# Row scatters given places behind the tiles' q work, and the gate weights' low halves formed on VectorE without a clamp

## The chip, the cores and the metric

The kernel runs on one core of a Trainium2 chip. The metric is the device time of one execution in microseconds (us); a run's time is one execution, and the kernel before has a median of 771.07 us over 3 runs (768.2 to 772.1). All times below come from one profiled execution of that kernel.

## The reference

Three stages follow each other on 3072 tokens of 384 numbers (4 batches of 768 tokens, 8 heads of 48).

```python
# 1. linear attention with decay
f = 1 / (1 + exp(-f_logit))
for t in range(768):
    state = f[:, :, t, :, None] * state + einsum('bhd,bhe->bhde', k[:, :, t], v[:, :, t])
    y[:, :, t] = einsum('bhd,bhde->bhe', q[:, :, t], state)
# 2. a skip score and one expert of 8 (w1: 384 x 1024, w2: 1024 x 384)
do = x @ w_skip > 0
e = argmax(x[do] @ w_gate);  p = its softmax share
out = x;  out[do] = x[do] + p * (relu(x[do] @ w1[e]) @ w2[e])
# 3. RMS norm and a gated layer (384 -> 1536 -> 384)
xn = x / sqrt(mean(x * x) + 1e-6) * rms_g
g = xn @ w_gate2
return (g * sigmoid(g) * (xn @ w_val2)) @ w_out2
```

The three weights of stage 3 (`g_gate`, `g_val`, `g_out` in the kernel) come as 64-bit floats, all else as 32-bit floats.

## The kernel before

Every product that needs 32-bit accuracy in stages 2 and 3 is made of 16-bit halves: a number is a high half (`hi`, `wgh`, `gh`, names in h) plus a low half (`lo`, `wgl`, `gl`, names in l), and TensorE (PE) multiplies hi by hi, hi by lo and lo by hi into one sum.

**Attention, 0 to about 166 us.** 24 tiles of 128 tokens, tile i is chunk i//4 of batch i%4. `tile_ops` lists the steps of a tile. ACT makes the decay factors `en` and `ep`; DVE makes `ks = k*en` and POOL makes `qs = q*ep` (its instruction is kept in the list `scaled`); PE transposes both (`ptk`, `ptq`), ACT copies the results to `Tk` and `Tq`; PE makes the scores `sc` and the output `py`. POOL also decays the running `state`, which ACT copies into `sbd` for `py`. A table of offsets per step and 3.09 units per tile (`II`) order the steps of all tiles in one list; a scheduler that simulates the program then sets the order on each engine, and `tc.issue_after(x)` keeps an instruction behind x in that order.

**Routing.** Tiles go through `route_ops` in groups (4, 4, 4, 4, 4, 2, 1, 1): DVE finds the expert, PE counts ranks (`prk`), DVE writes each token's slot. Then each tile's rows `xh`, with `meta` copied beside them, are scattered to the DRAM buffer `xs` by slot: one indirect DMA on POOL's queue for each tile. The scatters of a group are listed `RS` apart and not before `RS_AT`; for the first 8 tiles tile i's scatter also stands behind the `qs` of tile 10 + (i+1)//2. Every scatter waits for twelve writes of zero rows to `xs` that go out on SP's queue between the attention's loads.

**Experts, about 186 to 330 us.** For each of 8 experts 256 slots are read transposed (`exT`); `ph`, relu to `hh` and `hl`, `ey`. `start(0)` does the first 96 slots of expert 0 (`pa`, `eah`, `eal`) before the last rows are scattered. Two side queues go beside them: weights of later experts, then the gate and value weights of stage 3 (`gates`), and the rows: `first` makes the normalised rows `xn` of blocks 0 and 1 and transposes them by DMA into `xnT`; `middle` and `place` scatter the rest to `xnd`, from which `later` reads them.

**Gate weights.** `prep_in(nm, p)` loads one sixth of `g_gate` or `g_val` (768 KB) as pairs of 32-bit words into a staging buffer `st` (4 of them), makes 32-bit floats of them (`narrow`, with ACT's absolute value and DVE's clamp, shift and two merges into one of 2 buffers `fb`), scales them by `rms_g` (ACT, three pieces of 256 columns), rounds to the high half (ACT) and subtracts for the low half (POOL, line 430). `prep_out` does `g_out`, with the low half on DVE already.

**Gated layer.** Six blocks of 512 tokens and 12 column groups m. `up` makes `pwg` and `pwv` (9 matmuls each), ACT's `sg`, DVE's `hf`, ACT's `gh`, DVE's `gl`; `down` sums `po` over all m. Blocks 0 and 1 go through `pair` side by side, while the rest of the weights is prepared; blocks 2 to 5 through `block`. `bounds` checks that all values stayed inside the ranges that the fast path allows; if not, a slow general path runs behind it.

Of the kernel before, what the change touches and what calls it, by code (L numbers as in the profile page):

```python
# [32 lines left out]
FORCE = False  # L33
NONE = 4096
NPRE = 0
POOL_LO = True
WB = 3
FA = 1
EARLY = 20
# [23 lines left out]
ALT = 0  # L63
ALM = 0
AHM = 1
RS = 4.0
RS_AT = 37.0
CLEAR = 10
GATED = 8
FIRST = 17  # L70
GROUPS = (4, 4, 4, 4, 4, 2, 1, 1)
BUFS = {'xT': 3}
# [15 lines left out]
def fused_kernel(ctx, tc, q, k, v, f, w_skip, w_gate, w1, w2, g_gate, g_val, g_out, rms_g, out, dbg=None):  # L88
# [47 lines left out]
    dec = keep.tile([128, NT, 2 * HP], F32, name="dec")  # L136
    cnt = keep.tile([128, 2 * E + 1], F16, name="cnt")
    osum = keep.tile([128, NT], F32, name="osum")
    big = keep.tile([128, 2 + 2 * E + 3], F32, name="big")

    wr = keep.tile([128, HP, E + 1], F32, name="wr")
# [49 lines left out]
    def narrow(o, lo, hi):


        nc.scalar.activation(out=o.bitcast(F32), in_=hi.bitcast(F32), func=AF.Abs)
        yield
        nc.vector.tensor_scalar(out=o.bitcast(F32), in0=o.bitcast(F32), scalar1=2.0 ** -15 * 1.125, scalar2=2.0 ** 16 * 1.9375, op0=ALU.max, op1=ALU.min)
        nc.vector.tensor_scalar(out=o, in0=o, scalar1=3, scalar2=0x3FFFFFFF, op0=ALU.logical_shift_left, op1=ALU.bitwise_and)
# [210 lines left out]
    def raw(src, n, wide):  # L408
        st = stg.tile([128, n, wide, 2], I32, tag="st", name="st64")
        load(st, src)  # L410
        yield
        fb = stg.tile([128, n, wide], I32, tag="fb", name="fb", bufs=FB)
        yield from narrow(fb, st[:, :, :, 0], st[:, :, :, 1])
        return fb.bitcast(F32)

    def prep_in(nm, p):
        src = (g_gate if nm == "wg" else g_val).bitcast(I32)
        wide = F2 // 6
        w = yield from raw(src[:, 2 * p * wide:2 * (p + 1) * wide].rearrange("(k p) (f t) -> p k f t", p=128, t=2), KD, wide)
        hi, lo = gT[nm][p]  # L420
        for j in range(KD):
            if POOL_LO:
                nc.scalar.activation(out=w[:, j, :], in_=w[:, j, :], func=AF.Copy, scale=gsc[:, j:j + 1])
            else:
                nc.scalar.activation(out=hi[:, j, :], in_=w[:, j, :], func=AF.Copy, scale=gsc[:, j:j + 1])
                nc.vector.scalar_tensor_tensor(out=lo[:, j, :], in0=w[:, j, :], scalar=gsc[:, j:j + 1], in1=hi[:, j, :], op0=ALU.mult, op1=ALU.subtract)
        if POOL_LO:
            nc.scalar.copy(out=hi, in_=w)
            yield
            nc.gpsimd.tensor_tensor(out=lo, in0=w, in1=hi, op=ALU.subtract)  # L430
# [112 lines left out]
    with actx:  # L543
# [141 lines left out]
        def route_ops(g):  # L685
# [61 lines left out]
                nc.gpsimd.tensor_copy(out=cnt[:, E + 1:], in_=cnt[:, 0:E])  # L747
            counted.append(g)
            for b in range(n):
                yield "rs"  # L750
                i = i0 + b
                xh = xhs.pop(i)

                with tc.issue_after(scaled[min(CLEAR + (i + 1) // 2, len(scaled) - 1)]) if i < GATED else ExitStack():
                    nc.gpsimd.tensor_copy(out=xh[:, DM:], in_=meta[:, i, :])
                    sc = nc.gpsimd.indirect_dma_start(out=xs, out_offset=bass.IndirectOffsetOnAxis(ap=slot[:, i:i + 1].bitcast(U32), axis=0),  # L756
                                                      in_=xh, in_offset=None, bounds_check=NS + NTOK - 1, oob_is_err=False)
# [90 lines left out]


    hs2 = {}  # L850

    def up(blk, m, b0):
        need("in", m // 2)
        xT = xnT[blk]
        sl = slice(m % 2 * 128, m % 2 * 128 + 128)
        pp = []
        for a, nm in enumerate(("wg", "wv")):
            p = ps.tile([128, NB * 128], F32, **bank(b0 + a), name=f"p{nm}")
            hi, lo = gT[nm][m // 2]
            terms = [(hi[:, j, sl], xT[:, j, :]) for j in range(KD)]  # L860
            terms += [(hi[:, j, sl], xT[:, KD + j, :]) for j in range(KD)]
            terms += [(lo[:, j, sl], xT[:, j, :]) for j in range(KD)]
            for j, (w, x) in enumerate(terms):
                nc.tensor.matmul(p, lhsT=w, rhs=x, start=(j == 0), stop=(j == len(terms) - 1))  # L864
# [3 lines left out]
        nc.scalar.activation(out=sg, in_=pg, func=AF.Silu, scale=1.0 / SG)  # L868
        hf = gk.tile([128, NB * 128], F32, tag="hf", name="hf")
        nc.vector.scalar_tensor_tensor(out=hf, in0=pv, scalar=SH / SG, in1=sg, op0=ALU.mult, op1=ALU.mult)  # L870
# [61 lines left out]

    def bounds():
        NBIG = 2 + 2 * E + 3
        NC = 3 + NBIG
        NA = NC + 2 * E + 1
        bad = keep.tile([128, NC], F32, name="bad")
        vio = keep.tile([128, 4], F32, name="vio")
        tot = keep.tile([1, NA + NT], F32, name="tot")

        def worst(j, a, op, lim, red):
# [7 lines left out]
        nc.vector.tensor_scalar(out=bad[:, 3:NC], in0=big, scalar1=TINY, scalar2=None, op0=ALU.is_ge)  # L949
# [14 lines left out]
        beyond(0, 3, 127.5)  # L964
        beyond(3, NC, 0.5)
# [107 lines left out]
    def add(gen, key=None, rows=0):  # L1073
        sides[rows].append((gen, key))
# [115 lines left out]
```

## Time and profile before

| | us |
|---|---|
| median of 3 runs | 771.07 |
| the profiled execution's own time | 771.55 |
| its span | 769.8 |
| PE busy in the span | 717.0 |
| DVE busy | 417.0 |
| ACT busy | 362.6 |
| POOL busy | 218.3 |
| PE's largest waits: last rows of expert 0 | 8.2 |
| ... for `sg` ahead of stage 3 | 6.7 |
| ... for `Tk` in the attention, three waits | 6.3 |

A timeline row gives start, duration, engine, line, operation, written and read tiles, the count where equal neighbours are put together, and in brackets how long the engine stood idle before it and what released it. A row of stretches gives a window and for each engine its busy time and its count of instructions, then the clock that PE was granted (1.00 is full), the DMA engines' busy share and GB/s.

### The profile page before, as it was taken

The page shows a single profiled execution, that of the slowest core. Times are in us where ns is not written, and L with a number is a line of the kernel's source. Part 1 is how long each engine was busy: PE and PEld are TensorE (multiplying, and loading weights), DVE is VectorE, ACT ScalarE, POOL GpSimd, SP SyncE. Part 2 cuts the span into 40 slices and gives each one's busy share as a digit, 9 for nine tenths or more (in the row PEclk, how much of TensorE's full clock was granted, in tenths as well). Part 3 has the DMA queues.
Part 4 walks back from the last instruction along what each step waited for, and adds up shares of the span by engine and source line. Part 5 has one row for each costly group of instructions (what it writes and reads, how often), then busy time and mean ns, then how long its engine had stood idle before and what let it go on. Part 6 is the DMA issues. An engine that isn't in the chain of part 4 may idle for free.

```text
span 769.8 us, 14043 instructions
## 1 busy us (share of the span) xinstructions
PE 717.0 (93%) x5452; PEld 440.7 (57%) x5452; DVE 417.0 (54%) x879; ACT 362.6 (47%) x803; POOL 218.3 (28%) x286
## 2 busy tenths in 40 slices
PE   8999799895999878869999999999999999999995
PEld 4788688784766555534444565454454455455443
DVE  2788577794788888999999500222222222222230
ACT  5877478643677766787765310221321222222131
POOL 5221653541365656677220020100100020002002
PEclk9999999998999999989999999999999999999998
DMA  9999978745688998765332400100200030001001
GB/s 150 181 196 201 203 164 209 230 139 164 183 256 258 287 224 255 234 158 170 89 124 76 83 32 10 42 1 1 64 18 1 1 83 0 1 1 42 1 0 46
DMA packets 166459, 88.10 MB, mean 114 GB/s; under 512 B 137432, under 2 KB 151048, under 8 KB 166384
## 3 DMA queue, kind: packets, MB, share of 16 engines
q1 hardware_dynamic: 161904, 74.44, 40.5%
q0 software_dynamic: 4480, 12.67, 4.5%
q8 instruction: 45, 0.74, 0.4%
q14 instruction: 30, 0.25, 0.1%
HBM read 64.18 MB, written 16.24 MB: 104 GB/s over the span
## 4 chain that ended last, share of the span: by engine, by line
PE 70%; DMA 9%; DVE 7%; ACT 4%; POOL 3%; issue 3%; SPq 2%; POOLq 0%; ACTq 0%; DVEq 0%
PE po L887 18%; PE pwv L864 18%; PE pwg L864 18%; DMA xnd<-xn,at 3%; PE sc L641 3%; DMA st<-in_moe_w_dram 3%; PE py L657 2%; PE py L652 2%; SPq L573 1%; DVE w2l L405 1%; PE ptq L623 1%; PE ptk L623 1%; POOL xs L756 1%; PE pm L633 1%; PE px L678 1%
## 5 line engine op out<-in xcount | busy, mean ns | idle before, releaser
L870 DVE SCALAR_TENSOR_TENSOR hf<-pwv,sg 128x512 f32<-128x512 f32 x72 | 49.4, 688 | 180.2 <-PE pwv L864 158.8
L895 POOL DMA_INDIRECT out_dram<-ot,ids x24 | 24.2, 1010 | 337.3 <-ACT ot L894 332.7
L864 PE MATMUL pwg<-xnT,wgh 128*128 128x512 f16 x432 | 106.2, 382 | 6.7 <-ACT sg L868 6.7
L864 PE MATMUL pwv<-xnT,wvh 128*128 128x512 f16 x432 | 106.4, 381 | 0.0
L873 ACT CAST gh<-hf 128x512 f16<-128x512 f32 x72 | 44.3, 616 | 107.3 <-DVE hf L870 107.1
L887 PE MATMUL po<-wol,gh 128*128 128x384 f16 x288 | 93.7, 326 | 0.0
L887 PE MATMUL po<-woh,gh 128*128 128x384 f16 x288 | 93.7, 326 | 0.0
L887 PE MATMUL po<-woh,gl 128*128 128x384 f16 x288 | 93.4, 326 | 0.0
L868 ACT ACTIVATE sg<-pwg 128x512 f32<-128x512 f32 x72 | 42.6, 594 | 101.6 <-PE pwg L864 101.6
L887 PEld LDWEIGHTS <-gh 128*128 128x128 f16 x576 | 56.4, 98 | 41.8
L864 PEld LDWEIGHTS <-wgh 128*128 128x128 f16 x432 | 42.5, 98 | 54.5 <-issue 8.0
L864 PEld LDWEIGHTS <-wvh 128*128 128x128 f16 x432 | 42.5, 98 | 51.1 <-issue 1.6
L874 DVE TENSOR_TENSOR gl<-hf,gh 128x512 f16<-128x512 f32 x72 | 52.5, 729 | 35.4 <-ACT gh L873 35.4
L1011 PE MATMUL ph<-exT,w1h 128*128 128x256 f16 (+1 forms) x384 | 57.3, 275 | 8.2 <-DMA exT<-xs 8.2
L864 PE MATMUL pwg<-xnT,wgl 128*128 128x512 f16 x216 | 59.5, 383 | 0.0
L864 PE MATMUL pwv<-xnT,wvl 128*128 128x512 f16 x216 | 58.7, 379 | 0.0
L1011 PEld LDWEIGHTS <-w1h 128*128 128x128 f16 x432 | 40.4, 101 | 20.0 <-DMA exT<-xs 8.3
L604 POOL TENSOR_TENSOR qs<-q,ep 128x384 f32<-128x384 f32 x24 | 27.9, 1164 | 60.3 <-ACT ep L600 47.2
L1058 PE MATMUL ey<-w2h,hh 128*128 128x384 f16 x112 | 37.0, 331 | 8.0 <-ACT hh L1014 7.9
L894 ACT ACTIVATE ot<-po 128x384 f32<-128x384 f32 x24 | 11.6, 490 | 61.0 <-PE po L887 51.8
L887 PEld LDWEIGHTS <-gl 128*128 128x128 f16 x288 | 28.2, 98 | 18.6
L1058 PE MATMUL ey<-w2h,hl 128*128 128x384 f16 x112 | 31.3, 331 | 7.2 <-DVE hl L1015 5.2
(203 smaller groups left out, 1386.5 us busy)
## 6 DMA issues: line engine op xcount, KB each, us to landing
st<-in_moe_w_dram SPq DMA_DIRECT2D x32, 768.0 KB, 6.1
f<-in_f_logit_dram SPq DMA_DIRECT2D x24, 192.0 KB, 4.6
q<-in_q_dram SPq DMA_DIRECT2D x24, 192.0 KB, 4.3
k<-in_k_dram SPq DMA_DIRECT2D x24, 192.0 KB, 4.5
v<-in_v_dram SPq DMA_DIRECT2D x24, 192.0 KB, 4.5
st<-in_moe_w_gate_dram SPq DMA_DIRECT2D x6, 768.0 KB, 4.5
st<-in_moe_w_val_dram SPq DMA_DIRECT2D x6, 768.0 KB, 4.6
st<-in_moe_w_out_dram SPq DMA_DIRECT2D x6, 768.0 KB, 4.2
```

What stands on the lines that cost most here:

```text
L604: scaled.append(nc.gpsimd.tensor_tensor(out=qs[:, :, 0:D], in0=ins["q"], in1=ep, op=ALU.mult).ins)
L623: nc.tensor.transpose(pt[:, j, :], s[:, 2 * j:2 * j + 2, :].rearrange(flat), idf)
L641: nc.tensor.matmul(scs[r][:, j, :], lhsT=T["k"][64 * r:64 * r + 64, j, :], rhs=T["q"][64 * r:64 * r + 64, j, :], start=True, stop=True)
L864: nc.tensor.matmul(p, lhsT=w, rhs=x, start=(j == 0), stop=(j == len(terms) - 1))
L868: nc.scalar.activation(out=sg, in_=pg, func=AF.Silu, scale=1.0 / SG)
L870: nc.vector.scalar_tensor_tensor(out=hf, in0=pv, scalar=SH / SG, in1=sg, op0=ALU.mult, op1=ALU.mult)
L873: nc.scalar.copy(out=hh, in_=hf)
L874: nc.vector.tensor_tensor(out=hl, in0=hf, in1=hh, op=ALU.subtract)
L887: nc.tensor.matmul(po[t], lhsT=a[:, sl], rhs=w, start=(m == 0 and j == 0), stop=(m == KF2 - 1 and j == 2))
L895: sc = nc.gpsimd.indirect_dma_start(out=out, out_offset=bass.IndirectOffsetOnAxis(ap=at[:, t:t + 1].bitcast(U32), axis=0), in_=ot, in_offs ...
L1011: nc.tensor.matmul(out[:, i, :], lhsT=a, rhs=r, start=(j == 0), stop=(j == len(terms) - 1))
L1058: nc.tensor.matmul(py[t], lhsT=a[:, sl], rhs=w[:, m, :], start=(m == 0 and j == 0), stop=(m == KF - 1 and j == 2))
```

## The change

1. A tile's scatter is placed by the `qs` of a later tile: for the first 12 tiles that of tile 12 + (i+1)//2, for the others that of tile i + 6; the last six are free. `RS` falls from 4 to 1, and the list place is set by that tile too.
2. The gate and value weights' high half is written by the three scaling ACT instructions, and the low half by three DVE instructions of 256 columns; the ACT rounding and the POOL subtraction go.
3. For all 18 pieces of the 64-bit weights `narrow` runs without absolute value and clamp; the shift reads the staging buffer itself.
4. Instead, `ranges` loads all 18 pieces once more during blocks 2 to 4, takes the exponents with one DVE instruction, and their maximum and minimum with two more; `bounds` compares these with limits. Two of its steps are listed after each m, behind the newest `gl`.
5. ACT's table for stage 3 is loaded after expert 0, and not at the first `sg`.

```diff
-POOL_LO = True
+POOL_LO = False
-RS = 4.0
-RS_AT = 37.0
-CLEAR = 10
-GATED = 8
+RS = 1.0
...
+        src = hi
+        if clamp:
+            nc.scalar.activation(out=o.bitcast(F32), in_=hi.bitcast(F32), func=AF.Abs)
+            yield
+            nc.vector.tensor_scalar(... op0=ALU.max, op1=ALU.min)
+            src = o
+        nc.vector.tensor_scalar(out=o, in0=src, scalar1=3, scalar2=0x3FFFFFFF, op0=ALU.logical_shift_left, op1=ALU.bitwise_and)
...
-        yield from narrow(fb, st[:, :, :, 0], st[:, :, :, 1])
+        yield from narrow(fb, st[:, :, :, 0], st[:, :, :, 1], clamp=False)
...
+    def ranges():
+        j = 0
+        for source, n, wide in [in_source(nm, p) for nm in ("wg", "wv") for p in range(6)] + [out_source(p) for p in range(6)]:
+            st = stg.tile([128, n, wide, 2], I32, tag="st", name="st64")
+            nc.sync.dma_start(out=st, in_=source)
+            yield
+            fb = stg.tile([128, n, wide], I32, tag="fb", name="fb", bufs=FB)
+            nc.vector.tensor_scalar(out=fb, in0=st[:, :, :, 1], scalar1=20, scalar2=0x7FF, op0=ALU.logical_shift_right, op1=ALU.bitwise_and)
+            yield
+            nc.vector.tensor_reduce(out=expo[:, 0, j:j + 1], in_=fb, axis=AX.XY, op=ALU.max)
+            yield
+            nc.vector.tensor_reduce(out=expo[:, 1, j:j + 1], in_=fb, axis=AX.XY, op=ALU.min)
+            yield
+            j += 1
...
+                behind = 12 + (i + 1) // 2 if i < 12 else i + 6
+                turn[0] = II * behind + 4.5 if behind < NT else 0.0
                 yield "rs"
-                with tc.issue_after(scaled[min(CLEAR + (i + 1) // 2, len(scaled) - 1)]) if i < GATED else ExitStack():
+                with tc.issue_after(scaled[behind]) if behind < min(NT, len(scaled)) else ExitStack():
...
-            t = ... max(at + RS, RS_AT) if nm == "rs" ...
+            t = ... max(at + RS, turn[0]) if nm == "rs" ...
...
+        worst(3, expo[:, 0], ALU.is_le, 1150.0, ALU.max)
+        worst(4, expo[:, 1], ALU.is_ge, 897.0, ALU.min)
...
             run(expert(e), N2)
+            if e == 0:
+                with tc.issue_after(pins[-1][0]):
+                    nc.scalar.preload_act_table_set("silu_and_others")
...
+    add(ranges(), ("ranges",))
     for blk in range(2, NT // NB):
         if blk == NT // NB - 1:
+            need("ranges")
             checks = bounds()
         for m, _ in enumerate(block(blk)):
             if m == 4 and blk + 1 < NT // NB:
                 later(blk + 1)
+            with tc.issue_after(gated[-1]):
+                steps(N6)
```

The order of instructions shows three places. The first is POOL around the first scatters. Before, from the `qs` of tile 10 on (L604 is `qs`, L755 the copy of `meta`, L756 the scatter, L614 the state's decay; `qs_140` and `qs_141` are the two buffers that tiles take in turn):

```order
L604 TENSOR_TENSOR qs_140<-q,ep 128x8x48
L755 COPY xh<-meta 128x4
L614 TENSOR_TENSOR state<-state,e_1358 128x192
L756 DMA xs<-xh,slot 5120x388
L604 TENSOR_TENSOR qs_141<-q,ep 128x8x48
L755 COPY xh<-meta 128x4 x2
L614 TENSOR_TENSOR state<-state,e_1502 128x192
L756 DMA xs<-xh,slot 5120x388 x2
L604 TENSOR_TENSOR qs_140<-q,ep 128x8x48
```

And now, from the same `qs` on (its line is L629, the decay's L639, the copy's L782, the scatter's L783):

```order
L629 TENSOR_TENSOR qs_141<-q,ep 128x8x48
L639 TENSOR_TENSOR state<-state,e_1359 128x192
L629 TENSOR_TENSOR qs_142<-q,ep 128x8x48
L639 TENSOR_TENSOR state<-state,e_1499 128x192
L629 TENSOR_TENSOR qs_141<-q,ep 128x8x48
L782 COPY xh<-meta 128x4
L783 DMA xs<-xh,slot 5120x388
L639 TENSOR_TENSOR state<-state,e_1635 128x192
L629 TENSOR_TENSOR qs_142<-q,ep 128x8x48
L782 COPY xh<-meta 128x4 x2
L783 DMA xs<-xh,slot 5120x388 x2
```

The first scatter moved from the `qs` of tile 10 to that of tile 12, two tiles later. Further on it now is two scatters in each of tiles 13 to 17, one in tile 18, none in 19, three in 20, one in 21, none in 22 and the last eight behind tile 23; before there were one, two, two, two and one in tiles 10 to 14, four in tile 15, four more in a row some tiles later, and eight behind tile 23.

The second place is DVE at the end of the last expert. Before, from an expert's low half (L1015) behind the `x` of the row above it to the last `xn` (L472, `x_5327`) that the transposed rows of block 1 need; L196 to L201 are `narrow`:

```order
L1015 SCALAR_TENSOR_TENSOR hl<-ph,hh 128x256
L196 TENSOR_SCALAR fb<-fb 128x768
L197 TENSOR_SCALAR fb<-fb 128x768
L510 COPY ms_x<-m_5330 128x1
L199 SCALAR_TENSOR_TENSOR fb<-st_5730,fb 128x768
L490 TENSOR_SCALAR at<-exr 128x1
L487 SCALAR_TENSOR_TENSOR ms_x<-exr,m_5406 128x1
L201 SCALAR_TENSOR_TENSOR fb<-st_5730,fb 128x768
L488 COPY xn<-exr 128x4
L196 TENSOR_SCALAR fb<-fb 128x768
L197 TENSOR_SCALAR fb<-fb 128x768
L472 SCALAR_TENSOR_TENSOR xn<-x_5327,m_5330,xn 128x384
```

Now, from the same low half (L1045) to the same `xn` (here from `x_5329`, L495) and the three low halves of a weight behind it (L450); the `x` (L483) stands in between:

```order
L1045 SCALAR_TENSOR_TENSOR hl<-ph,hh 128x256
L483 SCALAR_TENSOR_TENSOR x_5376<-ey_5032,exr 128x384
L533 COPY ms_x<-m_5332 128x1
L199 TENSOR_SCALAR fb<-st_5754 128x768
L513 TENSOR_SCALAR at<-exr 128x1
L511 COPY xn<-exr 128x4
L495 SCALAR_TENSOR_TENSOR xn<-x_5329,m_5332,xn 128x384
L450 SCALAR_TENSOR_TENSOR wvl_118<-fb,gsc,wvh_117 128x256 x3
```

Between the expert's low half and that `xn` there now is one step of `narrow` (L199 is now the shift) instead of six.

The third place is DVE in blocks 2 and later, of which this piece stands for all. Before (L528 makes the row numbers of a block):

```order
L528 CAST ids<-idf__6819 128x4
L870 SCALAR_TENSOR_TENSOR hf<-pwv,sg 128x512
L528 CAST ids<-idf__7018 128x4
L874 TENSOR_TENSOR gl<-hf,gh 128x512
L870 SCALAR_TENSOR_TENSOR hf<-pwv,sg 128x512
```

And now (L898 is `hf`, L902 `gl`, L434 to L438 are `ranges`):

```order
L898 SCALAR_TENSOR_TENSOR hf<-pwv,sg 128x512
L902 TENSOR_TENSOR gl<-hf,gh 128x512
L434 TENSOR_SCALAR fb<-st_6920 128x768
L898 SCALAR_TENSOR_TENSOR hf<-pwv,sg 128x512
L902 TENSOR_TENSOR gl<-hf,gh 128x512
L436 TENSOR_REDUCE expo<-fb 128x1
L438 TENSOR_REDUCE expo<-fb 128x1
```

A piece of the check takes two `up`s: one has the exponents behind it, the next both reductions, ahead of the following `hf`.

More of the change, by code (lines that the diff above doesn't have):

```diff
@@ L47 @@
 N5 = 1
+N6 = 2
 HB = 24
@@ L138, in fused_kernel @@
     osum = keep.tile([128, NT], F32, name="osum")
+    expo = keep.tile([128, 2, 18], F32, name="expo")
     big = keep.tile([128, 2 + 2 * E + 3], F32, name="big")
@@ L189, in consts2, with narrow @@
         top(big[:, 1:2], wr_h[:, 0, 1:E + 1])
[L191 to L197, printed above, removed]
+    def narrow(o, lo, hi, clamp=True):
+        src = hi
+        if clamp:
+            nc.scalar.activation(out=o.bitcast(F32), in_=hi.bitcast(F32), func=AF.Abs)
+            yield
+            nc.vector.tensor_scalar(out=o.bitcast(F32), in0=o.bitcast(F32), scalar1=2.0 ** -15 * 1.125, scalar2=2.0 ** 16 * 1.9375, op0=ALU.max, op1=ALU.min)
+            src = o
+        nc.vector.tensor_scalar(out=o, in0=src, scalar1=3, scalar2=0x3FFFFFFF, op0=ALU.logical_shift_left, op1=ALU.bitwise_and)
         yield
@@ L412, in raw, with in_source, out_source, prep_in @@
         fb = stg.tile([128, n, wide], I32, tag="fb", name="fb", bufs=FB)
-        yield from narrow(fb, st[:, :, :, 0], st[:, :, :, 1])
+        yield from narrow(fb, st[:, :, :, 0], st[:, :, :, 1], clamp=False)
         return fb.bitcast(F32)
-    def prep_in(nm, p):
+    def in_source(nm, p):
         src = (g_gate if nm == "wg" else g_val).bitcast(I32)
         wide = F2 // 6
-        w = yield from raw(src[:, 2 * p * wide:2 * (p + 1) * wide].rearrange("(k p) (f t) -> p k f t", p=128, t=2), KD, wide)
+        return src[:, 2 * p * wide:2 * (p + 1) * wide].rearrange("(k p) (f t) -> p k f t", p=128, t=2), KD, wide
+    def out_source(p):
+        return g_out.bitcast(I32)[p * 256:(p + 1) * 256, :].rearrange("(k p) (d t) -> p k d t", p=128, t=2), 2, DM
+    def ranges():
[12 more added lines that the diff above has]
+            j += 1
+    def prep_in(nm, p):
+        w = yield from raw(*in_source(nm, p))
         hi, lo = gT[nm][p]
@@ L436, in prep_out @@
     def prep_out(p):
-        src = g_out.bitcast(I32)
-        w = yield from raw(src[p * 256:(p + 1) * 256, :].rearrange("(k p) (d t) -> p k d t", p=128, t=2), 2, DM)
+        w = yield from raw(*out_source(p))
         yield from split(oT[p][0], oT[p][1], w, SO, 1)
@@ L536, in fused_kernel @@
     scaled = []
+    turn = [0.0]
+    casts = []
     holds = []
@@ L749, in route_ops @@
             for b in range(n):
+                i = i0 + b
+                behind = 12 + (i + 1) // 2 if i < 12 else i + 6
+                turn[0] = II * behind + 4.5 if behind < NT else 0.0
                 yield "rs"
-                i = i0 + b
                 xh = xhs.pop(i)
-                with tc.issue_after(scaled[min(CLEAR + (i + 1) // 2, len(scaled) - 1)]) if i < GATED else ExitStack():
+                with tc.issue_after(scaled[behind]) if behind < min(NT, len(scaled)) else ExitStack():
                     nc.gpsimd.tensor_copy(out=xh[:, DM:], in_=meta[:, i, :])
@@ L823, in push @@
                 return
-            t = max(at, base + OFF[nm] + DOFF.get(nm, 0.0)) if nm in OFF else max(at + RS, RS_AT) if nm == "rs" else at + STEP[nm]
+            t = max(at, base + OFF[nm] + DOFF.get(nm, 0.0)) if nm in OFF else max(at + RS, turn[0]) if nm == "rs" else at + STEP[nm]
             seq[0] += 1
@@ L850, in fused_kernel @@
     hs2 = {}
+    gated = []
     def up(blk, m, b0):
@@ L873, in up @@
         nc.scalar.copy(out=hh, in_=hf)
-        nc.vector.tensor_tensor(out=hl, in0=hf, in1=hh, op=ALU.subtract)
+        gated.append(nc.vector.tensor_tensor(out=hl, in0=hf, in1=hh, op=ALU.subtract).ins)
         hs2[blk, m] = hh, hl
@@ L934, in bounds @@
         NBIG = 2 + 2 * E + 3
-        NC = 3 + NBIG
+        NC = 5 + NBIG
         NA = NC + 2 * E + 1
         bad = keep.tile([128, NC], F32, name="bad")
-        vio = keep.tile([128, 4], F32, name="vio")
+        vio = keep.tile([128, 5], F32, name="vio")
         tot = keep.tile([1, NA + NT], F32, name="tot")
@@ L948, in bounds @@
         worst(2, ms_x, ALU.is_ge, 1.0, ALU.min)
-        nc.vector.tensor_scalar(out=bad[:, 3:NC], in0=big, scalar1=TINY, scalar2=None, op0=ALU.is_ge)
+        worst(3, expo[:, 0], ALU.is_le, 1150.0, ALU.max)
+        worst(4, expo[:, 1], ALU.is_ge, 897.0, ALU.min)
+        nc.vector.tensor_scalar(out=bad[:, 5:NC], in0=big, scalar1=TINY, scalar2=None, op0=ALU.is_ge)
         pt = ps.tile([128, 512], F32, **bank(3), name="tot")
@@ L962, in beyond @@
                 nc.vector.tensor_scalar(out=o, in0=o, scalar1=(most - mid) ** 2, scalar2=None, op0=ALU.is_gt)
-        beyond(0, 3, 127.5)
-        beyond(3, NC, 0.5)
+        beyond(0, 5, 127.5)
+        beyond(5, NC, 0.5)
         beyond(NC, NC + E, LOW, CAP)
```

## Prediction, made before the change was run

> **What bounds the kernel now.** I read the page's head first, then PE's waits, then stretches of the span, then the rows of the two stretches in which PE stands.
>
> ```profile
> span 769.8 us, 14043 instructions
> PE ph L1011 <- DMA exT<-xs: 8.2, 1, 8.2
> PE pwg L864 <- ACT sg L868: 6.7, 1, 6.7
> PE ptq L623 <- ACT Tk L626: 6.3, 3, 4.8
> 78.00:86.00 8.00, 3.16 (x28) 2.85 (x24) 2.14 (x5) 4.08 (x11) 6.37 (x10) 0.79 0.98 214
> 86.00:166.00 80.00, 75.41 (x1124) 66.54 (x1124) 62.25 (x174) 55.92 (x137) 39.55 (x56) 1.00 0.75 192
> 300.00:345.00 45.00, 34.02 (x212) 20.89 (x211) 43.65 (x80) 34.23 (x76) 32.17 (x34) 0.93 0.72 214
> 345.00:480.00 135.00, 135.00 (x688) 67.72 (x687) 86.18 (x124) 63.75 (x122) 29.58 (x26) 0.99 0.30 84
> 480.00:770.00 290.00, 280.92 (x1448) 141.35 (x1445) 67.87 (x111) 67.48 (x134) 20.31 (x20) 0.99 0.07 20
> ```
>
> The columns of a stretch are PE, weight loads, DVE, ACT, POOL, then PE's clock. After 345 us PE has no gap until the output's end, so nothing that merely relieves another engine there can be worth anything. Time can only come from three places: the attention's gaps, the wait for the last scattered rows (8.2 us), and the end of the experts, where DVE is busy for 43.65 of 45 us and PE for 34. The median (771.07) lies 0.5 us under the profiled execution (771.55, of which 1.75 around the span); I work out differences from the one and take them off the other.
>
> **1. The scatters in the attention.**
>
> ```profile
> 72.82 1.75 SPq L776 DMA_DIRECT2D xs<-zero x2
> DMA to landing us min/median/max: 3.3/4.0/4.8
> 72.13 1.06 PE L652 MATMUL py<-Tq,sbd 128*128 128x128 f32 x8
> 66.43 1.28 POOL L604 TENSOR_TENSOR qs<-q,ep 128x384 f32<-128x384 f32 x1 [3.16 <-ACT ep L600]
> 78.87 1.20 POOL L756 DMA_INDIRECT xs<-xh,slot  x1 [10.31 <-DMA q<-in_q_dram]
> 81.30 0.49 POOL L614 TENSOR_TENSOR state<-state,e 128x192 f32<-128x192 f32 x1
> 83.29 1.09 PE L623 MATMUL ptq<-idf,qs 128*128 128x128 f32 x4 [4.84 <-ACT Tk L626]
> 84.17 1.92 PE L652 MATMUL py<-Tq,sbd 128*128 128x128 f32 x8
> 91.87 1.34 POOL L604 TENSOR_TENSOR qs<-q,ep 128x384 f32<-128x384 f32 x1 [2.74 <-ACT ep L600]
> 99.21 1.34 POOL L604 TENSOR_TENSOR qs<-q,ep 128x384 f32<-128x384 f32 x1 [2.74 <-ACT ep L600]
> 105.27 1.43 POOL L604 TENSOR_TENSOR qs<-q,ep 128x384 f32<-128x384 f32 x1 [2.74 <-ACT ep L600]
> 159.63 1.06 POOL L604 TENSOR_TENSOR qs<-q,ep 128x384 f32<-128x384 f32 x1 [3.60 <-ACT ep L600]
> ```
>
> The first two rows are the last zero writes on SP's queue and the landing of all twelve; the third is a `py` at full clock. The second of that pair leaves at about 74, and 4.8 us later, at 78.8, the first scatter starts, after POOL stood for 10.31 us. It was queued right behind tile 10's `qs` (66.43), so the next `qs`, the state's decay (81.30), ACT's copies behind that and PE's `ptq` (83.29, 4.84 us idle) all came late.
>
> From there on a loop POOL, ACT, POOL sets the pace: `qs`, scatters, decay, and 2.74 us in which POOL waits for ACT's next `ep`. Its period is 99.21 - 91.87 = 7.34 us with two scatters in a tile and 105.27 - 99.21 = 6.06 with one, so a scatter costs 1.28 (1.03 of itself and 0.3 of issue). Tiles 10 to 23 took 159.63 - 66.43 = 93.2 us.
>
> In the new order tile 10 and 11 have no scatter, 12 and 18 one, 13 to 17 two each, 20 three, 21 one, 19 and 22 none. With 6.06 for none or one, 7.34 for two and 8.62 for three that is 7 x 6.06 + 5 x 7.34 + 8.62 = 87.7 us: **5.5 us less**. Counting 6.06 also for a tile without a scatter is on the safe side for POOL, but PE needs about that much of its own: 93.2 us less its idle time here (4.84 in the one gap and 80 - 75.41 = 4.6 later) is 83.8 in 13 tiles, 6.4 each. PE's own work is also the far bound: 93.2 - 83.8 and the 0.9 by which the slow `py` (1.92 against 1.06) was longer make 10 us. The near bound is 0: nothing excludes that the pairs in five tiles in a row eat what the first wait gives back. The waiting rows take more staging: 13 buffers `xh` hold them, the scatters are up to two tiles later, and the buffer's next writer is DVE's copy for a tile eleven later; I see no wait there.
>
> The first scatter must find the zero writes landed. Two tiles of 6.06 after 66.43 and the `qs` itself (1.28) put it at about 79.8, 0.9 us behind 78.87. That is thin, and it is the first rival.
>
> **2. The last rows.** The 8.2 us end with the chain count, slot, scatter, transposed read:
>
> ```profile
> 179.00 1.19 POOL L756 DMA_INDIRECT xs<-xh,slot  x1 [1.51 <-DVE slot L732]
> 185.09 0.98 PE L1011 MATMUL ph<-exT,w1h 128*128 128x160 f16 x6 [8.21 <-DMA exT<-xs]
> L1015 DVE SCALAR_TENSOR_TENSOR eal<-pa,eah 128x384 f16<-128x384 f32 x2 | 1.1, 558 | 0.7 <-ACT eah L1014 0.7
> ```
>
> In the new order the last tile's slot stands ahead of the second `eal` on DVE and its `prk` about 15 matmuls of `pa` earlier on PE. One `eal` is 0.56, 15 matmuls at 0.98/6 at most 2.4, but PE's order overlaps with waits there; I take **1.0**, between 0 and 2.
>
> **3. The end of the experts.** This is where parts 2 and 3 of the change meet a limit:
>
> ```profile
> 333.00 3.63 DVE L196 TENSOR_SCALAR fb<-fb 128x768 f32<-128x768 f32 x1
> 332.82 0.92 POOL L458 TENSOR_TENSOR x<-xr 128x384 f32<-128x384 f16 x1
> 334.56 1.64 POOL L430 TENSOR_TENSOR wgl<-fb,wgh 128x768 f16<-128x768 f32 x1
> 337.35 2.44 POOL L467 TENSOR_TENSOR m<-m,mhalf 128x1 f32<-128x1 f32 x2
> 340.30 0.62 DVE L472 SCALAR_TENSOR_TENSOR xn<-x,m,xn 128x384 f16<-128x384 f32 x1
> 340.94 1.22 SPq L512 DMA_TRANSPOSE xnT<-xn  x1
> 341.58 1.28 ACT L868 ACT_TABLE_LOAD   x1
> 343.53 2.72 PE L864 MATMUL pwg<-xnT,wgh 128*128 128x512 f16 x6 [6.67 <-ACT sg L868]
> DMA to landing us min/median/max: 3.7/4.2/4.6
> 480.34 1.46 PE L864 MATMUL pwg<-xnT,wgh 128*128 128x512 f16 x6
> 345.00:350.00 5.00, 5.00 (x15) 1.85 (x14) 3.29 (x7) 4.05 (x9) 4.67 (x5) 0.62 0.90 271
> L196 DVE TENSOR_SCALAR fb<-fb 128x768 f32<-128x768 f32 x18 | 13.2, 733 | 0.7 <-ACT fb L194 0.4
> L1015 DVE SCALAR_TENSOR_TENSOR hl<-ph,hh 128x256 f16<-128x256 f32 x56 | 22.9, 415 | 2.1 <-ACT hh L1014 2.0
> ```
>
> One clamp took 3.63 us, five times its mean of 0.733, and it ended only when POOL had finished its sums and the low half begun at 334.56. Behind it stand the block's last `xn` (340.30), the transposes (340.94) and, in ACT's order, the table load. PE stood from 336.9 to 343.53 and then ran at 0.62 of its clock.
>
> Now the clamp is gone, and so is POOL's 1.64 ahead of the mean (`m`). The first `m` ended at 337.35 + 1.22 = 338.6 and now ends 1.64 earlier, near 336.9; the two halves of `xn`, on ACT and DVE, take 0.6 each (DVE's row), so the transposes leave at about 338.1 in place of 340.94. The new PE order wants block 1's rows first, which land 3.7 later (the least of the two landings here): 341.8, against 343.53. That is 1.7 us; the table load is no longer in the way. The clock costs 1.26 us in the first six matmuls (2.72, against 1.46 at full clock) and 5 x 0.38 = 1.9 in 345 to 350, which overlap: about 2.7. A gap of 4.9 is left, like the one at 83 us, whose `py` lost 0.9 and what followed some more: I leave 1.4 lost and take 1.3 as gained. Together **3.0**, between 0 and 8 (all of 6.67 and half of the clock).
>
> Against that stand 12 x 3 = 36 low halves on DVE: the nearest row has 0.415 us for 256 columns, 14.9 in all, against the 13.2 of the clamps. So DVE's load hardly changes; what changes is that the 3.63 and POOL's 1.64 are gone from this chain, and that by the order only one step of the conversion stands ahead of that `xn`. In 345 to 480 DVE has 49 us free for what is left.
>
> **4. What costs nothing.** The table load moves into ACT's gap ahead of a `hh` of expert 0 (1.17 idle, the load 1.28): 0.1 us of cost at most, taken. The second load of 13.8 MB and its 54 DVE instructions run beside blocks 2 to 4:
>
> ```profile
> L870 DVE SCALAR_TENSOR_TENSOR hf<-pwv,sg 128x512 f32<-128x512 f32 x48 | 33.2, 692 | 180.2 <-PE pwv L864 158.8 <-ACT sg L868 21.4
> L943 DVE TENSOR_REDUCE vio<-dec 128x1 f32<-128x192 f32 x1 | 0.3, 342 | 0.0
> L943 DVE TENSOR_REDUCE vio<-ms_x x1: 171/171/171, 363.1 to 363.1; 128x1 f32<-128x30 f32 x1
> ```
>
> The DMA engines are 7% busy there. A DVE instruction of 192 elements takes 0.342 and one of 30 takes 0.171, so 1.06 ns an element and 0.95 us for 768; twice 0.95 stand between a `gl` and the next `hf`. DVE waits 180 us in 48 turns, 3.7 each, so 1.9 fits. They decide from 1.9 a reduction on; the stretched clamp shows that an instruction can be five times its mean, but POOL has almost nothing to do here (20 us in 290). On SP's queue the 18 loads stand among the transposes of blocks 3 to 5; a load may wait there for a staging buffer that two `up`s (2 x 6.0 us: 48 in 288) free, while a block's rows are asked for m = 4 of the block before, 48 us ahead. Cost 0; the far end is in (c).
>
> **The sum.** 5.5 + 1.0 + 3.0 - 0.1 = 9.4 us: 771.55 becomes 762.15, the median 761.7.
>
> [...]
>
> **Rivals.** (a) The zero writes are still not down: the loads of the attention now come earlier as well, and the first scatter waits as before. Then the 4.84 us come back two tiles later: 766.5. For it: the margin of 0.9 us, and DMA engines 98% busy there. Against it: SP's zero writes stand where they stood. Chance 0.13. Of the same size is the case that five pairs in a row bring nothing.
>
> (b) The low halves on DVE take the place of the clamp: three of them, stretched as the clamp was, are 3 us ahead of the next `hf` or `xn`, and the third term goes: 764.7. For it: DVE is full until 345. Against it: in the order they stand behind the last `xn`, and POOL's own 1.64 is gone. Chance 0.18.
>
> (c) Slower: a reduction of 768 elements read in two dimensions takes 3 us, not 0.95. Then each second `hf` is 6.0 - 3.7 = 2.3 us late; PE has the next `pwg` in the other bank meanwhile, which I take for half of it, so about 1 us in each of 18 pieces is lost: 779.7. It decides from 1.9 on. For it: no reduction of this size is in the trace. Against it: 0.342 for 192. Chance 0.05.
>
> **How the numbers follow.** My forecast has 0.64, (a) 0.13, (b) 0.18, (c) 0.05. The range reaches from all three terms near their far bounds (10, 2 and 6.5 off the median: 752.5) to (a) and (b) together (769.5, cut to 769). A measurement of this kernel tells 0.5%, 3.9 us, from no change: faster means under 767.2. My own case, (b) alone and most of (a) lie under it; (a) and (b) together, or (a) with half of the first term, don't: 0.81 faster, 0.13 within, 0.06 slower.
>
> **What would show it.** Right: the first scatter is at 79 to 81 with little idle time before it and the wait of `ptq` for `Tk` falls from 6.3 to about 1.5; `qs` of the last tile is near 154; the wait of `pwg` falls from 6.7 to about 4.9 and is put down to a DMA; no PE gap from 480 on. Wrong: POOL waits for DMA near 79 again; DVE rows of the low halves at 1 us or more near 335; a reduction over 1.9 us.

## The result, and the profile after

| | before | changed |
|---|---|---|
| median of the runs (us) | 770.58 (768.2 to 772.1, 4 runs) | 761.99 (759.81 to 763.0, 4 runs) |
| ratio, 95% interval | | 0.9888 [0.9855, 0.9921] |
| the profiled execution's span | 769.8 | 760.2 |

The change makes the kernel faster by 8.6 us, where 9.4 was forecast. That sum is right, but its terms are not. PE's waits in the changed kernel:

```profile
PE ey L1088 <- ACT hh L1044: 8.1, 9, 3.0
PE ph L1041 <- DMA exT<-xs: 6.9, 1, 6.9
PE ey L1088 <- DVE hl L1045: 5.5, 7, 3.3
PE ptq L648 <- ACT Tk L651: 4.2, 5, 1.2
PE pwg L892 <- DMA xnT<-xn: 0.7, 1, 0.7
```

Each row has what PE waited for, the sum, the times and the longest. The wait ahead of stage 3 fell from 6.7 to 0.7; the attention's waits for `Tk` fell only from 6.3 to 4.2, now in five pieces of at most 1.2. In the experts the longest wait for `hh` is now 3.0 us, in expert 5, and the longest for `hl` 3.3, in expert 7. (Experts are counted from 0 here; the expectations below call expert 5 "expert 6".) The places are seen best as milestones, in the timelines of POOL, PE, DVE and SP's queue:

```profile
79.11 1.28 POOL L629 TENSOR_TENSOR qs<-q,ep 128x384 f32<-128x384 f32 x1 [4.13 <-ACT ep L625]
80.83 1.20 POOL L783 DMA_INDIRECT xs<-xh,slot  x1 [0.30 <-DMA v<-in_v_dram]
157.31 1.27 POOL L629 TENSOR_TENSOR qs<-q,ep 128x384 f32<-128x384 f32 x1 [4.33 <-ACT ep L625]
175.63 0.98 POOL L783 DMA_INDIRECT xs<-xh,slot  x1 [1.07 <-DVE slot L757]
181.52 0.98 PE L1041 MATMUL ph<-exT,w1h 128*128 128x160 f16 x6 [6.88 <-DMA exT<-xs]
284.55 0.50 PE L1088 MATMUL ey<-w2h,hh 128*128 128x384 f16 x1 [3.01 <-ACT hh L1044]
300.44 0.42 DVE L1045 SCALAR_TENSOR_TENSOR hl<-ph,hh 128x256 f16<-128x256 f32 x1
316.37 0.82 PE L1088 MATMUL ey<-w2h,hl 128*128 128x384 f16 x2 [3.34 <-DVE hl L1045]
323.52 0.41 DVE L1045 SCALAR_TENSOR_TENSOR hl<-ph,hh 128x256 f16<-128x256 f32 x1
333.64 1.22 SPq L535 DMA_TRANSPOSE xnT<-xn  x1
333.68 1.46 PE L892 MATMUL pwg<-xnT,wgh 128*128 128x512 f16 x6
336.49 1.46 PE L892 MATMUL pwg<-xnT,wgh 128*128 128x512 f16 x6 [0.70 <-DMA xnT<-xn]
344.25 1.46 PE L892 MATMUL pwv<-xnT,wvh 128*128 128x512 f16 x6
```

And those rows of before that the prediction does not show: expert 5's wait, the same two `hl` and the wait between them, and the third and eighth group of matmuls of stage 3:

```profile
288.11 0.34 PE L1058 MATMUL ey<-w2h,hh 128*128 128x384 f16 x1 [2.17 <-ACT hh L1014]
304.36 0.42 DVE L1015 SCALAR_TENSOR_TENSOR hl<-ph,hh 128x256 f16<-128x256 f32 x1
318.12 0.82 PE L1058 MATMUL ey<-w2h,hl 128*128 128x384 f16 x2 [2.33 <-DVE hl L1015]
324.62 0.41 DVE L1015 SCALAR_TENSOR_TENSOR hl<-ph,hh 128x256 f16<-128x256 f32 x1
334.75 1.46 PE L864 MATMUL pwg<-xnT,wgh 128*128 128x512 f16 x6
353.90 1.46 PE L864 MATMUL pwv<-xnT,wvh 128*128 128x512 f16 x6
```

| milestone | before | changed | gained so far |
|---|---|---|---|
| `qs` of tile 23 | 159.63 | 157.31 | 2.32 |
| last scatter | 179.00 | 175.63 | 3.37 |
| last rows of expert 0 reach PE | 185.09 | 181.52 | 3.57 |
| PE goes on in expert 5 | 288.11 | 284.55 | 3.56 |
| an `hl` in expert 6 | 304.36 | 300.44 | 3.92 |
| an `hl` in expert 7 | 324.62 | 323.52 | 1.10 |
| third group of stage 3 | 334.75 | 333.68 | 1.07 |
| eighth group of stage 3 | 353.90 | 344.25 | 9.65 |
| span | 769.8 | 760.2 | 9.6 |

So 3.6 us were gained up to the last rows, 2.5 were lost again in experts 6 and 7, and the step into stage 3 brought 8.6. From the eighth group to the end nothing moved. These are single executions: in a second profile of the changed kernel tile 23's `qs` started at 158.70 and the last rows came at 182.81, 1.4 and 1.3 later, with nearly the same span, 760.4.

### The profile page after: what moved, and what is told of

Read it like the earlier page. It is cut to its first block, busy times and chain, and to the rows that moved or that the text cites. A ratio compares the mean times of both kernels' runs of the same rounds, so it can differ in the third digit from the quotient of the medians.

```text
span 760.2 us, 14086 instructions
## 1 busy us (share of the span) xinstructions
PE 718.8 (95%) x5452; PEld 442.6 (58%) x5452; DVE 446.9 (59%) x955; ACT 340.0 (45%) x773; POOL 197.6 (26%) x274
## 4 chain that ended last, share of the span: by engine, by line
PE 73%; DMA 8%; DVE 6%; ACT 4%; POOL 4%; issue 3%; SPq 0%; POOLq 0%; ACTq 0%; DVEq 0%
PE po L915 18%; PE pwv L892 18%; PE pwg L892 18%; DMA xnd<-xn,at 4%; PE sc L666 3%; PE py L682 3%; DMA st<-in_moe_w_dram 3%; PE py L677 2%; PE ptq L648 1%; PE ptk L648 1%; DVE w2l L407 1%; PE pm L658 1%; PE lg L698 1%; PE px L703 1%; POOL xs L783 1%
## 5 line engine op out<-in xcount | busy, mean ns | idle before, releaser
L898 DVE SCALAR_TENSOR_TENSOR hf<-pwv,sg 128x512 f32<-128x512 f32 x72 | 49.6, 691 | 147.1 <-PE pwv L892 126.1
L902 DVE TENSOR_TENSOR gl<-hf,gh 128x512 f16<-128x512 f32 x72 | 49.9, 696 | 35.9 <-ACT gh L901 35.9
L629 POOL TENSOR_TENSOR qs<-q,ep 128x384 f32<-128x384 f32 x24 | 28.8, 1202 | 73.3 <-ACT ep L625 58.1
```

Source lines behind the costliest of these rows:

```text
L629: scaled.append(nc.gpsimd.tensor_tensor(out=qs[:, :, 0:D], in0=ins["q"], in1=ep, op=ALU.mult).ins)
L902: gated.append(nc.vector.tensor_tensor(out=hl, in0=hf, in1=hh, op=ALU.subtract).ins)
```

## The experiments

Twelve kernels ran in three groups; those of a group share their runs of the kernel before. At the start, theory A read the milestones as they stand, with the loss put down to expert 5; theory B kept the prediction's split; rival C, within the second part, held that POOL's lost work is what counts and not the shorter conversion.

**The scatters alone.** The kernel before with part 1, of which this is the main line:

```diff
-                with tc.issue_after(scaled[min(CLEAR + (i + 1) // 2, len(scaled) - 1)]) if i < GATED else ExitStack():
+                with tc.issue_after(scaled[behind]) if behind < min(NT, len(scaled)) else ExitStack():
```

> The kernel before with the new places of the row scatters and nothing else. Theory A (from the milestones of the two traces: expert 0's rows begin 3.6 us earlier, and a clock slowed behind a 3.0-us gap in expert 6 takes some 2.5 of it back): expert 0's last rows at about 181.5 in place of 185.1, the time 1 to 3.6 us under before, 767 to 770. Theory B (the prediction's own split): the scatters carry 6.5 us, 764. Either way the 4.84-us gap near 83 us is gone.

Measured: 766.57, ratio 0.9952 [0.9929, 0.9975], 3.7 us with an interval of 1.9 to 5.5. B's 6.5 lies outside it; A's range of 1 to 3.6 lies mostly inside, with the median just past its end. In its profile the scatters left PE's wait for `sg` as it was, 6.6 us. But A's reason for the loss is not borne out there: PE stood 2.95 us in expert 5, and the gain at the `hl` of expert 6 behind it was still 5.64 (298.72).

**The weights alone.** The changed kernel with the old constants and the old `issue_after` of the scatters.

> The changed kernel with the scatters back in their old places; the weights' conversion, second load, checks and table load as changed. Theory A: the gain of the end of the experts is 8 to 9 us and does not need the scatters; 762 to 764, with PE's wait ahead of stage 3 under 1.5 us. Theory B: that part is worth 3.0 us, 768.

Measured: 763.38, ratio 0.9912 [0.9883, 0.9941], 6.8 us, in A's range. 3.7 and 6.8 make 10.5, and both together gave 8.6; the intervals allow a plain sum, and no run tells whether the two take something from each other.

**The low half back on POOL, still without a clamp.** The constant also brings back ACT's separate rounding.

```diff
-POOL_LO = False
+POOL_LO = True
```

> The changed kernel, but the low half of the gate and value weights on POOL again (and the high half by ACT's rounding); no clamp. Theory A: what frees the end of the experts is the shorter conversion, which gives staging buffers back sooner, so SP's queue reaches the row load behind them sooner; POOL's 1.7-us subtraction beside DVE gives part of it back: 763 to 766. Rival C: the gain comes from POOL standing idle (no two-input work beside DVE); then 768 or more.

Measured: 772.76, ratio 1.002 [0.9997, 1.0044]. The whole gain is gone, the scatters' too. A had it wrong. SP did issue the last row load of block 1 early (321.70, as in the changed kernel with 321.80, and not 326.38), so the early load alone does not bring the gain. What DVE and POOL did there (DVE first):

```profile
331.69 3.98 DVE L199 TENSOR_SCALAR fb<-st 128x768 int32<-128x768 int32 x1
337.71 0.55 DVE L199 TENSOR_SCALAR fb<-st 128x768 int32<-128x768 int32 x1
331.88 0.92 POOL L481 TENSOR_TENSOR x<-xr 128x384 f32<-128x384 f16 x1
332.75 0.92 POOL L484 TENSOR_TENSOR x<-x,exr 128x384 f32<-128x384 f32 x1
333.62 1.63 POOL L454 TENSOR_TENSOR wvl<-fb,wvh 128x768 f16<-128x768 f32 x1
343.65 1.22 SPq L535 DMA_TRANSPOSE xnT<-xn  x1
```

With the clamp gone it was the shift that took 3.98 us in place of 0.55: it began with POOL's run of two sums and the subtraction and ended 0.4 us behind it. The last transpose left at 343.65; in the changed kernel it left at 333.64.

**The clamp kept, low halves on DVE.** With the clamp the second load isn't needed, and this kernel leaves it out.

```diff
-        yield from narrow(fb, st[:, :, :, 0], st[:, :, :, 1], clamp=False)
+        yield from narrow(fb, st[:, :, :, 0], st[:, :, :, 1], clamp=True)
```

> The changed kernel with absolute value and clamp kept in the conversion, and so without the second load and its checks; low halves on DVE, new scatters. Theory A: the conversion has its old length and 0.4 us a piece more on DVE for the low halves; the row load comes late again and most of the gain at the end of the experts is lost: 767 to 770. Rival C (POOL standing idle is what counts): 762 to 764.

Measured: 760.92, ratio 0.9867 [0.9837, 0.9897]. All of the gain is there with the clamp. Together with the kernel ahead of it, this leaves rival C: the low half's way off POOL carries the second part. Taking out the clamp brought nothing that these runs can show: without clamp and without second load the ratio is 0.9853 [0.9825, 0.9881] (below).

**POOL kept busy with work that nobody needs.** The changed kernel with one idle subtraction for each piece at POOL's old place (`at` and `m` are not touched, no one reads `idle`), and another with two idle copies:

```diff
+            idle = stg.tile([128, KD, F2 // 6], F16, tag="idle", name="idle", bufs=1)
+            nc.gpsimd.tensor_tensor(out=idle, in0=hi, in1=hi, op=ALU.subtract)
```

Theory C1 puts what the old low half cost down to POOL's time in its queue ahead of the rows' sums and means; with the subtraction it expects 767 to 772.

> The changed kernel plus one idle POOL subtraction of two inputs (768 columns, the high half from itself, into a buffer that nobody reads) for each gate and value piece, at the place where POOL made the low half. Nothing waits for its result. [...] Theory C2 (what cost was the wait for the low half itself, or the buffer it held): 762.

> The same with two idle POOL copies of one input (768 columns each) in place of the subtraction, so that POOL is busy for about as long. If POOL's queue is what costs (C1), it is like the subtraction, 767 to 772 if the two copies take some 1.7 us. If the contention of two-input work with VectorE is what costs, VectorE's rows stay unstretched and it is 762 to 765.

Measured: 773.32, ratio 1.0052 [1.0031, 1.0074], and 781.36, ratio 1.0153 [1.0119, 1.0187]; the changed kernel beside them had 0.9889. A group of POOL in each of the two:

```profile
L458 POOL TENSOR_TENSOR idle<-wgh 128x768 f16<-128x768 f16 x6 | 9.8, 1628 | 14.4 <-ACT wgh L449 14.4
L459 POOL COPY idle<-wgh 128x768 f16<-128x768 f16 x12 | 14.4, 1198 | 1.6 <-ACT wgh L449 1.2
```

The subtraction of 1.6 us, with no reader, undoes everything, and by a little more than the 767 to 772 expected. The copies with one input, 2.4 us for a pair, cost more still, so a second input is not needed for the loss. How POOL's work does it, these runs do not separate. Three ways are seen. The sums and means of the rows stand behind the idle work in POOL's queue, and behind its wait for ACT's high half (14.4 us in all in the first row, but 1.6 in the second). DVE's instructions are stretched; a low half has 0.47 us at 328.23 in this profile, and 1.65 here, beside the idle subtraction of 1.47 (POOL first):

```profile
332.50 1.47 POOL L458 TENSOR_TENSOR idle<-wvh 128x768 f16<-128x768 f16 x1 [2.31 <-ACT wvh L449]
332.60 1.65 DVE L450 SCALAR_TENSOR_TENSOR wvl<-fb,gsc,wvh 128x256 f16<-128x256 f32 x1
```

And DVE's order differs. The scheduler simulates the program with the idle work in it, and it puts more of the conversion ahead of the last `xn` of block 1. Between the last `hl` of the experts and that `xn` there are 1 step of `narrow` in the changed kernel, 3 with the clamp kept, 5 with the idle subtraction, 6 with the low half on POOL and 6 before, 12 with the idle copies. The last transposes leave at 333.64, 335.18, 342.02, 343.65, 340.94 and 351.09. So part of the loss may be the schedule's, and no kernel here has the old work on POOL with the new order on DVE.

**The first scatter one tile earlier.**

```diff
-                behind = 12 + (i + 1) // 2 if i < 12 else i + 6
+                behind = 11 + (i + 1) // 2 if i < 12 else i + 6
```

> The changed kernel with each of the first 12 scatters one tile earlier (behind the q work of tile 11 + (i+1)//2). Theory A: the first scatter then stands at about 73.9 us in POOL's queue, before the last zero rows land at 78.8, POOL waits nearly 5 us and PE has a gap of 3 to 5 us again: the time is 2 to 4 us above the changed kernel, 764 to 766. Rival D: the wait for the zero rows was not what cost, only the number of scatters in a tile: 762.

Measured: 763.22, ratio 0.987 [0.9831, 0.9909], not to be told from the changed kernel. Its profile shows the mechanism, though:

```profile
77.99 1.20 POOL L783 DMA_INDIRECT xs<-xh,slot  x1 [4.24 <-DVE xh L706]
81.23 0.63 PE L648 MATMUL ptq<-idf,qs 128*128 128x128 f32 x4 [3.07 <-ACT Tk L651]
```

POOL stood 4.24 us and PE 3.07 again, at a clock of 1.00 over 78 to 86 us, and the last rows reached PE at 183.49, 2.0 us later than in the changed kernel. Later scatters stood one tile earlier, and what that gave back is not told apart here. That the wait is for the zero rows is argued from the kernel's dependency and from the times; the profile puts it down to others.

**The table load at its old place.**

```diff
-            if e == 0:
-                with tc.issue_after(pins[-1][0]):
-                    nc.scalar.preload_act_table_set("silu_and_others")
```

> The changed kernel with ACT's table loaded at the first sg again. Theory A: PE now waits 0.7 us for block 1's rows there and not for sg, so 1.3 us on ACT ahead of the first sg costs 0 to 1.3: 762 to 763.3. Rival F: it is on the path in full and delays the chain behind it too: 764 or more.

Measured: 761.16, ratio 0.9859 [0.9821, 0.9897]: no cost, at the lower end of what A allowed (762 to 763.3). From the last transposes to the end its profile takes 426.6 us, as that of the changed kernel does.

**No second load.** The exponents' instructions and their DMAs left out:

```diff
-    add(ranges(), ("ranges",))
+    nc.vector.memset(expo, 1000.0)
```

> The changed kernel without the second load of the weights and its 54 VectorE instructions (the exponents' check is left out: a constant stands in its place). Theory A: all of it lies in blocks 2 to 5 beside a PE without gaps, so it costs nothing: 761.5 to 762.5. Rival G: its DMA traffic or DVE time costs in blocks 2 to 5, and without it the time is 760 or less, as that of the kernel that kept the clamp and had no second load (760.9).

Measured: 760.59, ratio 0.9853 [0.9825, 0.9881], against 0.9888 and 0.9889 for the changed kernel in other groups. The point lies 2.7 us lower and the intervals overlap, so a small cost is not excluded by the times. The traces put none of it where the second load runs:

```profile
329.31 1.22 SPq L535 DMA_TRANSPOSE xnT<-xn  x1
```

From these last transposes to the end of the span (755.9) it is 426.6 us, and in the changed kernel from 333.64 to 760.2 it is 426.6 too. What differs stands ahead of them: expert 5's wait is 0.95 us instead of 3.01.

**Expert 5's wait.** DVE stands there until a row scatter has given a buffer back, 3.1 us in the changed kernel. First 4 buffers for the addresses and 3 for the rows in place of 2 each, then more:

> The changed kernel with 4 buffers for the row addresses (at) and 3 for the normalised rows (xn) in place of 2. Theory A: the 3.0-us gap of PE in expert 6 comes from DVE waiting for a scatter's DMA to give such a buffer back, and the half clock behind it costs 2 to 3 us more; both go: 757 to 760. Rival E: the rows behind it wait for something else at the same place, and nothing changes: 762.

Measured: 759.1, ratio 0.9817 [0.9785, 0.9849]. The theory fell in its profile: the wait did not go, it moved from the address to the row and was longer. DVE and then PE:

```profile
283.71 0.17 DVE L511 COPY xn<-exr 128x4 f32<-128x4 f32 x1 [4.25 <-DMA xnd<-xn,at]
284.26 0.50 PE L1088 MATMUL ey<-w2h,hl 128*128 128x384 f16 x2 [4.15 <-DVE at L513]
```

So this ratio does not come from there. What the profile shows in its place: no step of `narrow` stands between the last `hl` and the last `xn`, and the last transposes left at 331.83, 1.8 us earlier than in the changed kernel; its span is 2.3 shorter. With 6 and 5 buffers, beside the changed kernel itself:

```diff
-        xn = nk.tile([128, ROW], F32, tag="xn", name="xn")
+        xn = nk.tile([128, ROW], F32, tag="xn", name="xn", bufs=5)
-        at = nk.tile([128, 1], I32, tag="at", name="at")
+        at = nk.tile([128, 1], I32, tag="at", name="at", bufs=6)
```

> The changed kernel itself, beside the kernels of this group: 760 to 763. PE's gap in expert 6 follows the landing of one row scatter (9.7 us in one profile, 6.8 in another kernel's) and so differs from run to run by 2 to 3 us.

> The changed kernel with 6 buffers for the row addresses and 5 for the normalised rows. With 4 and 3 the wait for the slow scatter only moved from the address to the row. Theory A: with 5 rows in flight no step waits for it, the gap of 1 to 4 us in expert 6 and the half clock behind it go: 756 to 759. Rival E: the rows' way is held elsewhere (SP's queue, POOL's sums) and it stays within 1 us of the changed kernel.

Measured: 761.6 (0.9889 [0.9858, 0.9921]) for the changed kernel and **755.74** (0.9817 [0.9785, 0.985]) with the buffers, 5.9 us less in the same group and the fastest of all. PE's row in expert 5, stretches of 4 us there with the clock after POOL's busy time, and for comparison those of the changed kernel's first profile:

```profile
279.89 0.34 PE L1088 MATMUL ey<-w2h,hh 128*128 128x384 f16 x1 [0.60 <-ACT hh L1044]
280.00:284.00 4.00, 4.00 (x29) 2.60 (x28) 4.00 (x9) 3.16 (x8) 2.85 (x3) 1.00 1.03 263
284.00:288.00 4.00, 4.00 (x36) 3.11 (x34) 4.00 (x11) 3.87 (x11) 2.48 (x4) 1.00 1.07 230
```

```profile
280.00:284.00 4.00, 1.55 (x13) 1.04 (x11) 0.97 (x3) 0.98 (x3) 0.26 (x1) 0.95 0.76 89
284.00:288.00 4.00, 3.45 (x12) 1.71 (x13) 2.61 (x10) 2.24 (x9) 1.98 (x2) 0.50 0.50 170
288.00:292.00 4.00, 4.00 (x23) 2.69 (x22) 2.68 (x7) 4.00 (x8) 1.91 (x4) 0.69 1.09 228
```

Without the wait PE and DVE are full there and the clock stays at 1.00; in the changed kernel PE lost 3.0 us and then ran at 0.50 and 0.69. In the two profiles of this group DVE's rows around the wait, from one `hl` in expert 5 to one in expert 6, take 9.0 us (276.99 to 285.99) in place of 13.5 (279.96 to 293.49): 4.5 of the gain stand there.

## Why the prediction came out right, point by point

**The sum** was right (761.7 against 761.99) by luck, because its errors cancel: the scatters and last rows were put 2.9 us too high, the end of the experts 5.6 too low, and a loss of 2.5 in between was not seen. Of the signs that it named, the first scatter came at 79 to 81 and no PE gap came from 480 on; the wait for `Tk` (4.2, not 1.5), the last `qs` (157.31, not 154) and the wait of `pwg` (0.7, not 4.9) missed.

**The scatters: the term of 5.5 was mis-sized; it measured 2.3** at tile 23's `qs` and, with the last rows, 3.6 where 6.5 stood (0.9 and 2.3 in the second profile). The mechanism held: the first scatter started at 80.83 after 0.30 us, the margin of 0.9 us behind the zero rows was enough, and the gap of 4.84 is gone. The step that failed is the sum of the periods, 87.7 us; they took 91.0. The five pairs took 7.3 to 7.4 each, as priced. Tile 11 took 6.74 and not 6.06, and above all the tile with three scatters took 10.53 and not 8.62:

```profile
134.67 1.00 POOL L629 TENSOR_TENSOR qs<-q,ep 128x384 f32<-128x384 f32 x1 [2.23 <-ACT ep L625]
137.68 1.03 POOL L783 DMA_INDIRECT xs<-xh,slot  x1 [1.54 <-issue]
139.01 1.46 POOL L783 DMA_INDIRECT xs<-xh,slot  x1 [0.30 <-PE ptk L648]
140.77 1.76 POOL L783 DMA_INDIRECT xs<-xh,slot  x1 [0.30 <-issue]
145.20 1.07 POOL L629 TENSOR_TENSOR qs<-q,ep 128x384 f32<-128x384 f32 x1 [2.13 <-ACT ep L625]
145.65 1.16 PE L666 MATMUL sc<-Tq,Tk 64*128 64x128 f32 x16 [2.62 <-ACT Tq L651]
```

Such scatters in a row, of 1.44 and 1.75, already stood in the trace of before, in its second run of four; I priced all at 1.03. PE waits 2.62 us there, as it waited 2.90 before.

**The last rows: 1.0 forecast, 1.25 measured** (3.57 less 2.32).

**The end of the experts: the term of 3.0 was mis-sized; it measured 8.6,** more than its far bound of 8. I took one chain apart, the mean behind POOL's 1.64 and DVE's 3.63, and left the row where it came in. But the row came earlier too: its load left at 321.80 and not at 326.38, and POOL's first sum on it started at 328.03 and not at 332.82. So the last `xn` was made at 333.00, and the transposes left at 333.64, not at 338.1. PE's gap was 0.7 instead of the 4.9 that I left, and the clock, for which I counted 1.4 as lost, was 1.00 behind it (337.2 to 341.2). I also gave the clamp a share; the kernels with the clamp kept and with the low half back on POOL show that POOL's share is what counted. What stretched the clamp to 3.63 is not shown; its row has one input, and it ended 0.4 us behind POOL's run.

**The loss of 2.5 us was in no term.** I took the expert phase as moved and otherwise alike, and DVE's load as hardly changed. Between the two `hl` of the milestones the gain falls from 3.92 to 1.10. DVE has almost no idle time there (0.4 us before, 0.3 now), and it runs 14 steps of the conversion, 9.8 us with the six new low halves, where it ran 7 in 7.2 us before. The kernels of the experiments agree: with the scatters alone it is 7 steps and the gain there goes from 5.64 to 4.97; with the weights alone 14, from 2.13 to 0.07; with the low half back on POOL 7, from 4.04 to 4.50; with the clamp kept 10, from 4.06 to 3.84. So the loss goes with low halves on DVE and no clamp, when more of the conversion falls into this stretch; this is read from the traces, and no kernel was made to test it. The second part's net is then some 6 us (8.6 less 2.5), near the 6.8 that it measured alone.

**Expert 5's wait** is in no term either, but it is not that loss: behind it the gain was still there. In the changed kernel one scatter of rows to `xnd`, issued at 273.32, came down 9.7 us later, at 283.03. Behind PE's gap of 3.01 there its clock was 0.50 (284 to 288); before, behind 2.17 at the same place, it was 1.00 (288 to 292). The 1.4 us that the prediction left as lost behind a gap of 4.9 are its author's estimate; with a gap of 0.7 the case did not come up. Another 0.93 us of idling ended 2.1 us ahead of the gap of 3.01; whether that counts no run here tells.

**What costs nothing** held: a reduction took 0.946 us, where 0.95 was estimated, the exponents 0.555, PE has no gap from 345 to 752, and the table load is not to be seen.

**The rivals.** (a) and (c) did not come, with the margin and the price as worked out. (b) was half there: three low halves took 2.07 us at 327.97 in place of 1.27, but ahead of no `xn` that PE waited for; what the low halves did cost, they cost earlier, in experts 6 and 7.

## What to carry to other kernels

Where an engine is full for tens of microseconds, look at what the other engines run beside it: here twelve idle instructions of 1.6 us on POOL, with the order that the scheduler made around them, cost 11.7 us, more than the whole change brought. Where a scheduler sets the order, compare the orders too, or the experiment moves more than its edit says. When a wait is taken away in a stretch of linked chains, follow every row back to its load and not only the last chain, and give a run of queued scatters the durations of the worst run in the trace (here 1.44 and 1.75 us, where 1.03 was priced). Count the clock behind a gap of PE as well as the gap: in expert 5 of the changed kernel the gap was 3.0 us and the clock behind it 0.50 and then 0.69, and the kernel with three more buffers for rows and four more for addresses, where the gap is 0.6 and the clock 1.00, took 5.9 us less.

## What the runs showed of the hardware that was not expected

- One DVE instruction beside a run of POOL instructions took 3.6 to 4.0 us (3.63 before, 3.98 with the low half back on POOL) instead of 0.55, ending 0.4 us behind that run; idle copies with one input on POOL slowed the kernel (781.36) no less than a subtraction with two (773.32), though DVE's order differs too.
- The landing of one row scatter at the same place took 9.7 us in one profile and 6.8 in another kernel's (the one with the table load back), and PE's gap followed it (3.01 and 0.88).
- At the same place in expert 5, PE's clock over the 4 us behind its gap was 0.50 after 3.01 us, 0.57 after 2.75, 0.59 after 2.95, 0.65 after 2.52 and 0.68 after 2.27, in five profiles, and 1.00 after 2.17, 2.37 and 2.56 in three others; around 3.07 in the attention (first scatter earlier, 78 to 86 us) it was 1.00. So in these profiles the length of the single gap does not decide it. The 4 us behind 2.27 (idle copies), 2.52 (first scatter earlier) and 2.56 (clamp kept):

```profile
283.00:287.00 4.00, 3.86 (x17) 1.99 (x18) 2.19 (x9) 1.90 (x6) 2.02 (x2) 0.68 0.81 239
286.28:290.28 4.00, 4.00 (x19) 2.46 (x20) 2.49 (x10) 2.24 (x7) 2.51 (x3) 0.65 0.74 219
283.44:287.44 4.00, 4.00 (x28) 2.59 (x29) 2.49 (x10) 2.24 (x7) 2.51 (x3) 1.00 0.64 212
```
